# Turning batch 2 by DMA and loading batch 1 ahead of the second channel weight, in a sliding-window attention and MLP-mixer kernel

## The chip, the cores and the metric

The kernel runs on one core of a Trainium2 chip. Its time is the device time of one execution in microseconds (us), as the median of several runs. The engines are named as the profile names them: PE multiplies matrices (PEld loads its weights), DVE and ACT do elementwise work and read the matmul results out of PSUM, POOL does elementwise work on SBUF only, and SP issues most of the DMAs. POOL issues those DMAs that change fp32 weights to fp16 on the way. Each engine works through its own instructions in the order in which the program gives them, and waits for another engine or a DMA by a semaphore.

## The reference

Eight batches, eight heads, 576 positions of 64 elements. Half of the heads look back over a window of 32 positions, the other half over 128 positions in steps of four. The attention output is the input of an MLP mixer: a product over the positions, then one over the channels, each with a ReLU between two weights and a sum with its input.

```python
scores = scale * np.matmul(q, k.transpose(0, 1, 3, 2))
mask_plain = (rel >= 0) & (rel < 32)
mask_dil = (rel >= 0) & (rel < 128) & (rel % 4 == 0)
attn = softmax(where(mask, scores, -1e9));  x = attn @ v
h = np.maximum(xt @ w_tok1, 0.0) @ w_tok2          # positions
u = x + h.transpose(0, 2, 1)
out = u + np.maximum(u @ w_ch1, 0.0) @ w_ch2       # channels
```

The inputs are fp32; the kernel multiplies in fp16.

## The kernel before

The program has a start-up (batch 0's attention and position product, with nothing beside it) and then eight iterations, one for each batch `b`. The backbone of iteration `b` is the channel product of batch `b` on PE: twelve blocks `gp` (line 717, four matmuls of 512 columns each, a ReLU of each into `gt`), in odd iterations three small blocks `gt` and a block `yp` for the tails of two batches (lines 708 and 756), and four blocks `yp` against the second channel weight `w4` (line 736, 24 matmuls of 256 columns each). Into this backbone the program sets the attention and the position product of later batches. `interleave` does so by a table: each piece of side work has a place `t` on a counted time, and the pieces and the backbone are written out in that order. So the order on every engine is fixed when the program is built; the places are no waits.

A batch's side work is: loads of q, k and v (`l_q`, `l_k`, `lt` for the last 64 rows, `l_vn`, `l_vt`, `l_vd`, `l_vx`) issued by SP; casts to fp16 on POOL (`c_q`, `c_k`, `c_t`, `vv`, `vt`); q and k turned so that the head dimension lies on the partitions; scores, their exponentials on ACT (`attp` for the plain heads, `attd` for the dilated, `attt` for the last 64 queries); values (`av`, then `rec` and `xn` on DVE); position product (`h1p`, `up`, `u`); and `u` turned for the channel product (`uT`).

There are two ways to turn and to score. Batches 0 to 2 are turned by PE (`transposes`, line 310) and copied from PSUM; their scores are matmuls over 128 rows, in which the other head's rows are zero (`qz`). For batches 0 and 1 the mask is added by a further matmul (`veil`); for batch 2 POOL multiplies by the mask after the exponential. Batches 3 to 7 (`by_dma`) are turned by five DMA transposes on SP (`tt`, `qt`, `kr`, `qt`, `kr`; `qt` and `kr` are the places of q and k, two head pairs each time), POOL copies k into its place (`kt`, `place_steps`), and `scores_twin` computes two heads at once, each over 64 rows of PE, in two groups: group 0 for the plain heads, group 1 for the dilated. POOL multiplies by the masks after them. Their `u` is turned by a DMA transpose too (`turned`), into `utm`; ACT copies half of it into `utd` (line 649).

Loads are held back by a `gate`: a copy of one element on POOL into the tile that the first load writes, which can only run when the weight it reads has landed. Before the change the pieces of the first channel weight `w3` are loaded first, then a gate, the three pieces of `w4`, a gate on the first of them, and then batch 1.

Of the kernel before, what the change touches and what calls it, by code (L numbers as in the profile page):

```python
# [35 lines left out]
TW = 320  # L36
# [32 lines left out]
def kernel(  # L69
# [81 lines left out]
    w3a = fixed("w3", [128, 4, DCH])  # L151
    w3 = [w3a[:, i] for i in range(4)]
# [190 lines left out]
    def by_dma(b):  # L343
        return b >= 3
# [51 lines left out]
    def veiled(b, hp):  # L396
        return b <= 1
# [68 lines left out]
    def scores_twin(b, g):  # L466
# [35 lines left out]
        def main(hp):  # L502
            for h in range(2):
                p = ps[2 * (hp % 2) + h]
                if g == 0:
                    exp(plain_blocks(hp)[:, h, 0:3, 0:BLK].rearrange("p b (m r) -> p b m r", r=4),
                        p[:, 0:3 * BLK].rearrange("p (b r m) -> p b m r", r=4, m=40))
                else:
                    exp(attd[hp - 2][:, h], p)

        def rest():
            for h in range(2):
                p = small[h]
                if g == 0:
                    exp(attpa[:, :, h, 3 * PST:3 * PST + 128].rearrange("p a (m r) -> p a m r", r=4),
                        p[:, 256:512].rearrange("p (a r m) -> p a m r", a=2, r=4))
                t = attt[:, 2 * g:2 * g + 2, h, 64:TW].rearrange("p a (x c) -> p a x c", c=128)[:, :, :, 0:64]
                exp(t, p[:, 0:256].rearrange("p (a x c) -> p a x c", x=2, c=64))
# [9 lines left out]
        main(2 * g)  # L528
        if g:
            mask(2)  # L530
        main(2 * g + 1)
        if g:
            mask(3)
        rest()
        if not g:
            mask(0)
# [3 lines left out]
        if not g:  # L540
            mask(1)
# [89 lines left out]
    def turned(b):  # L631
        return b >= 3
# [18 lines left out]
    def score_steps(b, t0, dt, offs=(0.0, 0.7, 2.0), places=None):  # L651

        steps = []
        if by_dma(b):
            for g in range(2):
                for i, f in enumerate([scores_twin(b, g)] * 2):
                    steps.append((t0 + g * dt, 0.86 * (i == 0), lambda f=f: next(f)))
            return steps
        for hp in range(4):
# [4 lines left out]
            for i in range(3):  # L664
                steps.append((at_s + offs[i], 0.21, lambda g=g: next(g)))
# [30 lines left out]
    def gen_main(b):  # L696
# [4 lines left out]
        def w3_block(cb, mb):  # L701
            return w3[cb][:, 512 * (mb // 4) + mb % 4:512 * (mb // 4) + 512:4]
# [11 lines left out]
        for mb in range(NMB):  # L714
# [5 lines left out]
            relu(nc.vector if (mb % 2 == 1 if b == 0 else mb in (1, 5)) else nc.scalar, gta[:, mb, m0:m0 + 512], p)  # L720
# [86 lines left out]
    def load_w3(i):  # L807
        c = slice(512 * i, 512 * i + 512)
        nc.gpsimd.dma_start(out=w3a[:, :, c], in_=moe_w_ch1[:, c].rearrange("(x p) c -> p x c", p=128))
# [12 lines left out]
    nc.gpsimd.dma_start(out=w1p, in_=moe_w_tok1[0:512, :].rearrange("(m r) j -> m r j", r=4))  # L822
# [9 lines left out]
    load_w3(2)  # L832
# [90 lines left out]
    gate(w4a[0:1, 0, 0:1], w3[0][0:1, 512:513])  # L923
    for i in range(3):
        nc.gpsimd.dma_start(
            out=w4a[:, 4 * i:4 * i + 4],
            in_=moe_w_ch2[512 * i:512 * i + 512, :].rearrange("(p i) c -> p i c", i=4))
    gate(l32[(1, "t")][0:1, 0, 0:1], w4[0][0:1, 0:1])
    for nm in ("q", "k"):
        load_tail(1, nm, nc.sync)  # L930
    for h0 in (0, 4):
        for nm in ("q", "k"):
            load_qk(1, nm, h0, h0 + 4, nc.sync)
    casts1 = cast_steps(1)
    for i in (0, 1, 2, 3, 4, 5, 7, 6, 8):
        casts1[i]()
    load_v(1)
    new_qk(2)
    for nm in ("q", "k"):
        load_tail(2, nm, nc.sync)  # L940
    for nm in ("q", "k"):
        load_qk(2, nm, 0, 4, nc.sync)
# [4 lines left out]
    for b in range(B):  # L947
        steps = []
        if b == 0:
            steps += score_steps(1, 0, 0, (0.0, 0.6, 1.3),  # L950
                                 ((12.6, 14.8), (14.0, 16.8), (16.2, 18.6), (17.6, 20.2)))
            steps += at(18.6, 0.35, casts1[9:])
            steps += at(20.0, 0.0, [lambda nm=nm: load_qk(2, nm, 4, 8, nc.sync) for nm in ("q", "k")])
            steps += at(24.0, 0.0, [lambda: load_v(2)])
            casts = cast_steps(2)
            va = value_steps(1, 20.3, 0.7)
            steps += va[:4] + [(p + 0.2, c, f) for p, c, f in va[4:]]
            steps += mix_steps(1, 24.2, 27.0, 29.0, 34.8, 1.1)
            steps += score_steps(2, 0, 0, (0.0, 0.7, 1.6),
                                 ((28.8, 31.4), (31.2, 34.6), (0, 0), (0, 0)))[:10]  # L960
            steps += at(24.5, 0.5, casts[:9]) + at(34.5, 0.3, casts[9:])
            steps += at(36.0, 0.0, [lambda: emit_loads_qk(3)])
        elif b == 1:
            late = score_steps(2, -4.3, 2.4, (0.0, 0.7, 1.6))
            va = value_steps(2, 4.2, 1.0)
            steps += late[10:] + va[:4] + [(9.6 + (0.0, 0.8, 2.8, 3.6)[i], c, f) for i, (_, c, f) in enumerate(va[4:])]
# [44 lines left out]
```

## Time and profile before

| | |
|---|---|
| median of three runs | 293.93 us (293.59 to 293.98) |
| profiled execution | 293.95 us |
| its span, first to last instruction | 292.2 us |
| PE / PEld busy | 95% / 73% |
| DVE / ACT / POOL busy | 46% / 46% / 57% |
| DMA queue of SP, share of 16 engines | 64.8% |

The span begins with the first instruction of the kernel; 1.75 us of the profiled execution lie around it. The eight iterations begin at about 28.6, 69.7, 108.7, 138.1, 172.5, 201.2, 235.6 and 261.9 us. PE is busy nearly all the time, but its busy time is modelled and contains the tails of matmuls that overlap; what it loses is seen better in the waits and in the times at which its groups start.

### The profile page before, as it was taken

To read this page: it belongs to the slowest core of one execution; us is meant where nothing else is said; L and a number is where in the kernel's file an instruction comes from. 1 tells how busy PE (TensorE), PEld (TensorE's weight loads), DVE (VectorE), ACT (ScalarE), POOL (GpSimd) and SP (SyncE) were. 2 spreads that over 40 slices of the span, in tenths; PEclk is the share of its full clock that TensorE was granted. 3 is DMA by queue.
4 is the path that set the end of the run, shared out by engine and by line. 5 is a ranking of instruction groups with operands and counts; after the bars stand their busy time and mean duration, and the time that the engine had idled before them with its cause. 6 is when DMAs were issued, how large, how long until landed. Compare 5 with 4: busy or idle time off the path is not lost.

```text
span 292.2 us, 7087 instructions
## 1 busy us (share of the span) xinstructions
PE 278.1 (95%) x2850; PEld 213.4 (73%) x2850; DVE 133.2 (46%) x279; ACT 134.3 (46%) x266; POOL 166.3 (57%) x227
## 2 busy tenths in 40 slices
PE   5879999997999999999999999999999999999994
PEld 2677579985776896688766986697776966886593
DVE  7847338754844237413741245415540274422022
ACT  2854336347644614465347705482346524234500
POOL 7982056436999399739952998469952930000000
PEclk9999999999999999999999999999999999999999
DMA  8999999989938995869897989389775220431032
GB/s 222 271 202 190 206 323 210 328 220 276 245 64 183 306 264 131 103 118 329 238 181 139 326 208 217 73 210 336 193 145 100 84 72 2 90 111 36 2 90 91
DMA packets 103473, 52.12 MB, mean 178 GB/s; under 512 B 71792, under 2 KB 102384, under 8 KB 103440
## 3 DMA queue, kind: packets, MB, share of 16 engines
q1 hardware_dynamic: 99200, 46.55, 64.8%
q0 software_dynamic: 2640, 3.94, 7.7%
q10 hardware_dynamic: 1600, 1.18, 1.4%
q8 instruction: 22, 0.36, 0.5%
q14 instruction: 11, 0.09, 0.1%
HBM read 37.07 MB, written 9.44 MB: 159 GB/s over the span
## 4 chain that ended last, share of the span: by engine, by line
PE 84%; DMA 6%; POOL 5%; ACT 1%; SPq 1%; DVE 1%; issue 1%; POOLq 0%
PE yp L736 28%; PE gp L717 27%; PE h1p L579 5%; PE yp L756 4%; PE up L591 4%; PE gt L708 3%; DMA l_q<-in_q_dram 3%; DMA w1p<-in_moe_w_tok_dram 2%; PE sc L476 2%; PE h1p L577 1%; PE av L560 1%; PE up L602 1%; POOL vv L102 1%; PE av L555 1%; POOL attp L112 1%; DMA l_vd<-in_v_dram 1%
## 5 line engine op out<-in xcount | busy, mean ns | idle before, releaser
L736 PE MATMUL yp<-w,gt 128*128 128x256 f16 x756 | 86.9, 273 | 0.0
L106 ACT ACTIVATE gt<-gp 128x512 f16<-128x512 f32 x76 | 45.4, 597 | 84.4 <-PE gp L717 84.1
L736 PEld LDWEIGHTS <-gt 128*128 128x128 f16 x768 | 78.4, 106 | 6.5 <-issue 0.3
L717 PEld LDWEIGHTS <-w 128*128 128x128 f16 x384 | 40.0, 114 | 23.7 <-issue 1.5
L112 POOL TENSOR_TENSOR attp<-attp,const 128x1280 f16<-128x1280 f16 x12 | 31.3, 2611 | 33.7 <-ACT attp L500 27.5
L746 DVE TENSOR_TENSOR o<-yp,u 128x512 f32<-128x512 f32 x31 | 21.4, 691 | 62.3 <-PE yp L736 59.0
L717 PE MATMUL gp<-utd,w 128*128 128x512 f16 x120 | 45.5, 380 | 0.0
L717 PE MATMUL gp<-utm,w 128*128 128x512 f16 x120 | 45.5, 379 | 0.0
L717 PE MATMUL gp<-uT,w 128*128 128x512 f16 x144 | 36.3, 379 | 0.7 <-ACT uT L100 0.7
L112 DVE TENSOR_TENSOR xn<-av,rec 128x320 f16<-128x320 f32 x64 | 31.5, 492 | 2.2
L112 POOL TENSOR_TENSOR attd<-attd,const 128x1024 f16<-128x1024 f16 x12 | 25.3, 2123 | 0.0
L102 POOL CAST c_q<-l_q 128x512 f16<-128x512 f32 x31 | 19.7, 638 | 4.2 <-DMA l_q<-in_q_dram 4.2
L597 DVE TENSOR_TENSOR u<-up,xn 128x512 f16<-128x512 f32 x26 | 18.0, 691 | 8.1 <-PE up L591 8.1
L102 POOL CAST c_k<-l_k 128x512 f16<-128x512 f32 x29 | 17.7, 613 | 3.6 <-PE yp L736 1.8
L108 DVE TENSOR_SCALAR gt<-gp 128x512 f16<-128x512 f32 x20 | 13.8, 689 | 11.7 <-PE gp L717 11.2
L106 ACT ACTIVATE h<-h1p 128x256 f16<-128x256 f32 x29 | 11.1, 384 | 16.5 <-PE h1p L579 16.4
L568 DVE RECIPROCAL rec<-av 128x5 f32<-128x5 f32 x64 | 12.2, 190 | 13.2 <-PE av L565 12.7
L367 POOL COPY kt<-kr 128x512 f16<-128x512 f16 x10 | 10.8, 1078 | 7.9 <-DMA kr<-c_k 5.4
L500 ACT ACTIVATE attp<-sc 128x480 f16<-128x480 f32 (+1 forms) x30 | 13.4, 526 | 2.1 <-PE sc L476 2.1
L112 POOL TENSOR_TENSOR attt<-attt,const 128x512 f16<-128x512 f16 (+1 forms) x14 | 14.2, 1015 | 0.0
L393 PEld LDWEIGHTS <-kt 128*128 128x128 f16 x144 | 11.8, 103 | 3.2 <-issue 1.6
L606 DVE TENSOR_TENSOR u16t<-up,xn 64x512 f16<-64x512 f32 x7 | 4.8, 690 | 19.8 <-PE up L602 19.8
(136 smaller groups left out, 478.8 us busy)
## 6 DMA issues: line engine op xcount, KB each, us to landing
out_dram<-o SPq DMA_DIRECT2D x72, 128.0 KB, 3.4
l_q<-in_q_dram SPq DMA_DIRECT2D x15, 512.0 KB, 7.1
l_k<-in_k_dram SPq DMA_DIRECT2D x14, 512.0 KB, 7.3
l_vn<-in_v_dram SPq DMA_DIRECT2D x32, 128.0 KB, 5.3
l_vd<-in_v_dram SPq DMA_DIRECT2D x16, 256.0 KB, 4.7
w<-in_moe_w_ch_dram POOLq DMA_DIRECT2D x6, 512.0 KB, 7.6
lt<-in_q_dram SPq DMA_DIRECT2D x8, 128.0 KB, 4.5
l_vt<-in_v_dram SPq DMA_DIRECT2D x8, 128.0 KB, 4.1
```

Of the source, the lines that this page charges most:

```text
L102: eng.tensor_copy(out=out, in_=in_)
L106: nc.scalar.activation(out=out, in_=in_, func=AF.Relu)
L108: eng.tensor_scalar_max(out=out, in0=in_, scalar1=0.0)
L112: eng.tensor_tensor(out=out, in0=x, in1=y, op=ALU.mult)
L393: nc.tensor.matmul(out=out, lhsT=lhsT, rhs=qz[hp][:, h, queries], start=hide is None, stop=True)
L500: nc.scalar.activation(out=out, in_=in_, func=AF.Exp, scale=0.125)
L568: nc.vector.reciprocal(out=rec[:, :, 0], in_=av[:, :, 64])
L579: nc.tensor.matmul(out=p, lhsT=w[:, s, j], rhs=x[:, s, c], start=False, stop=(s == 3))
L597: nc.vector.tensor_tensor(out=u16(b, s), in0=blocks4(p), in1=blocks4(xn[b][:, s]), op=ALU.add)
L717: nc.tensor.matmul(out=p, lhsT=w3_block(cb, mb), rhs=uT[(b, cb)][0], start=(i == 0), stop=(i == 3))
L736: nc.tensor.matmul(out=p[:, c], lhsT=gta[:, mb, a0:m0 + 512:4] if half else gta[:, mb, a0:a0 + 128], rhs=w4[mb][:, c], start=(mb == 0), st ...
L746: nc.vector.tensor_tensor(out=blocks4(o32), in0=blocks4(p), in1=u16(b, s), op=ALU.add)
```

## The change

Batch 2 joins those that are turned by DMA (`by_dma` and `turned` from 2 on). Its scores move from the end of iteration 0 and the first third of iteration 1 to two places among the `gp` blocks of iteration 1, group 0 after the first block. The exponentials of `scores_twin` become single steps and begin with the small bank. The ReLUs of iteration 1 move in the greater part to DVE.

Batch 1 is loaded before `w4`: its gate now reads the second copy of `w2p` instead of `w4`. The third piece of `w3` is issued on POOL after two of batch 1's casts, the three pieces of `w4` after nine of them; `w3` is split into three tiles for that. Batch 1's transposes and scores move from the `yp` blocks of iteration 0 to its `gp` blocks, and its values and position product follow earlier. Batch 2's loads stand together, behind a gate on the second piece of `w4`. In the start-up, `w1p` is issued ahead of two casts.

```diff
     def by_dma(b):
-        return b >= 3
+        return b >= 2
...
     def turned(b):
-        return b >= 3
+        return b >= 2
...
+        def small_exps(h):
+            if g == 0:
+                last_blocks(h)
+                yield 0.0
+            tails(h)
+            yield 0.0
+
+        yield from small_exps(1)
+        for hp in (2 * g, 2 * g + 1):
+            for h in range(2):
+                main(hp, h)
+                if g and h:
+                    mask(hp)
+                yield 0.0
+        yield from small_exps(0)
+        if g == 0:
             mask(0)
...
-            relu(nc.vector if (mb % 2 == 1 if b == 0 else mb in (1, 5)) else nc.scalar, gta[:, mb, m0:m0 + 512], p)
+            relu(nc.vector if (mb % 2 == 1 if b == 0 else mb % 4 != 3 if b == 1 else mb in (1, 5)) else nc.scalar, gta[:, mb, m0:m0 + 512], p)
...
+    nc.gpsimd.dma_start(out=w1p, in_=moe_w_tok1[0:512, :].rearrange("(m r) j -> m r j", r=4))
+    for hp in range(2, 4):
+        cast_qk(0, "q", hp, nc.gpsimd)
     nc.gpsimd.dma_start(out=w1t[0][0:64], in_=moe_w_tok1[512:S, :])
     nc.gpsimd.tensor_copy(out=spread[:, 3:515:4], in_=ident)
-    for hp in range(2, 4):
-        cast_qk(0, "q", hp, nc.gpsimd)
-    nc.gpsimd.dma_start(out=w1p, in_=moe_w_tok1[0:512, :].rearrange("(m r) j -> m r j", r=4))
...
-    load_w3(2)
...
     new_qk(1)
-    gate(w4a[0:1, 0, 0:1], w3[0][0:1, 512:513])
-    for i in range(3):
-        nc.gpsimd.dma_start(
-            out=w4a[:, 4 * i:4 * i + 4],
-            in_=moe_w_ch2[512 * i:512 * i + 512, :].rearrange("(p i) c -> p i c", i=4))
-    gate(l32[(1, "t")][0:1, 0, 0:1], w4[0][0:1, 0:1])
+    gate(l32[(1, "t")][0:1, 0, 0:1], w2p[1][0:1, 0, 0:1])
...
+    load_v(1)
     casts1 = cast_steps(1)
-    for i in (0, 1, 2, 3, 4, 5, 7, 6, 8):
+    for i in (0, 1):
         casts1[i]()
-    load_v(1)
+    load_w3(2)
+    for i in (2, 3, 4, 5, 7, 6, 8):
+        casts1[i]()
+    for i in range(3):
+        nc.gpsimd.dma_start(
+            out=w4a[:, 4 * i:4 * i + 4],
+            in_=moe_w_ch2[512 * i:512 * i + 512, :].rearrange("(p i) c -> p i c", i=4))
+    for cast in casts1[9:]:
+        cast()
+
     new_qk(2)
+    gate(l32[(2, "t")][0:1, 0, 0:1], w4[4][0:1, 0:1])
     for nm in ("q", "k"):
         load_tail(2, nm, nc.sync)
-    for nm in ("q", "k"):
-        load_qk(2, nm, 0, 4, nc.sync)
+    for h0 in (0, 4):
+        for nm in ("q", "k"):
+            load_qk(2, nm, h0, h0 + 4, nc.sync)
+    load_v(2)
...
-            late = score_steps(2, -4.3, 2.4, (0.0, 0.7, 1.6))
-            va = value_steps(2, 4.2, 1.0)
...
-            steps += mix_steps(2, 10.8, 14.6, 17.2, 22.2)
-            steps += score_steps(3, 25.2, 4.2) + at(9.0, 0.6, cast_steps(3))
...
+            va = value_steps(2, 9.4, 0.95)
+            steps += score_steps(2, 0.6, 5.2, lag=0.5)
...
+            steps += mix_steps(2, 14.6, 18.4, 20.8, 32.8)
+            steps += score_steps(3, 27.0, 4.5) + at(9.0, 0.6, cast_steps(3))
```

Three places show how this moves the instructions. The first is POOL, from the end of the start-up on; the first number in a name is the number of the batch (`lt_1` belongs to batch 1). Before:

```order
L835 COPY w2p_1_83<-w2_81 128x512
L805 COPY w4_85<-w3_84 1x1
L925 DMA w4_85<-in_moe_w_ch2_dram 128x2048 x3
L805 CAST lt_1_583<-w4_85 1x1
L102 CAST c_t_1_595<-lt_1_583 128x512
L102 CAST c_q_1_597<-l_q_1_0_579 128x512
L102 CAST c_k_1_599<-l_k_1_0_581 128x512
```

Now:

```order
L842 COPY w2p_1_83<-w2_81 128x512
L813 CAST lt_1_584<-w2p_1_83 1x1
L102 CAST c_t_1_604<-lt_1_584 128x512
L102 CAST c_q_1_606<-l_q_1_0_580 128x512
L817 DMA w3_2_86<-in_moe_w_ch1_dram 128x4x512
L102 CAST c_k_1_609<-l_k_1_0_582 128x512
L102 CAST c_q_1_606<-l_q_1_0_580 128x512
L102 CAST c_k_1_609<-l_k_1_0_582 128x512
L102 CAST c_q_1_606<-l_q_1_1_581 128x512 x2
L102 CAST c_k_1_609<-l_k_1_1_583 128x512 x2
L944 DMA w4_87<-in_moe_w_ch2_dram 128x2048 x3
```

The gate of batch 1 stands ahead of all of `w4`, and the last third of `w3` and all of `w4` stand behind casts that wait for batch 1's data. After the rows shown come batch 1's casts of v, and only then the gate of batch 2.

The second place is SP's queue around batch 2's loads of v. Before:

```order
L191 DMA l_k_2_1_622<-in_k_dram 128x4x256
L752 DMA out_0_dram<-o32_0_2_906 128x256 x2
L208 DMA l_vn_2_1044<-in_v_dram 128x4x64 x4
L208 DMA l_vt_2_1047<-in_v_dram 64x8x64
L208 DMA l_vd_2_1045<-in_v_dram 128x2x256 x2
L208 DMA l_vx_2_1046<-in_v_dram 128x4x64
L752 DMA out_0_dram<-o32_0_3_1107 128x256 x2
L197 DMA lt_3_1275<-in_q_dram 64x8x64
```

Now:

```order
L207 DMA l_vd_2_641<-in_v_dram 128x2x256 x2
L207 DMA l_vx_2_642<-in_v_dram 128x4x64
L760 DMA out_0_dram<-o32_0_0_1016 128x256 x2
L348 DMA_TRANSPOSE tt_68<-c_t_2_1062 128x4x128
L760 DMA out_0_dram<-o32_0_1_1085 128x256 x2
L348 DMA_TRANSPOSE qt_66<-c_q_2_1064 128x8x128
L348 DMA_TRANSPOSE kr_67<-c_k_2_1081 128x8x128
L348 DMA_TRANSPOSE qt_66<-c_q_2_1064 128x8x128
L348 DMA_TRANSPOSE kr_67<-c_k_2_1081 128x8x128
L760 DMA out_0_dram<-o32_0_2_1153 128x256 x2
```

Batch 2's five transposes are new, and they stand behind all fourteen loads of the batch and behind the output of the first two blocks of iteration 0.

The third place is POOL in iteration 1, where k is put in place and the masks are applied. Before:

```order
L112 TENSOR_TENSOR attp_73<-attp_73,const_61 128x8x160
L112 TENSOR_TENSOR attt_76<-attt_76,const_61 128x2x2x64
L102 CAST vv0_69<-l_vn_2_1044 128x4x64 x4
L102 CAST vv0_69<-l_vt_2_1047 64x8x64
L102 CAST vv0_69<-l_vd_2_1045 128x4x2x64
L112 TENSOR_TENSOR attp_73<-attp_73,const_61 128x8x160
L112 TENSOR_TENSOR attt_76<-attt_76,const_61 128x2x2x64
```

Now:

```order
L366 COPY kt_65<-kr_67 128x512
L363 COPY kt_65<-tt_68 128x4x64
L366 COPY kt_65<-kr_67 128x512
L369 COPY kt_65<-kr_67 128x128 x2
L112 ISA
L112 TENSOR_TENSOR attp_73<-attp_73,const_61 128x8x160
L112 TENSOR_TENSOR attt_76<-attt_76,const_61 128x4x2x64
L112 TENSOR_TENSOR attp_73<-attp_73,const_61 128x8x160
L112 TENSOR_TENSOR attd0_74<-attd0_74,const_61 128x1024
L112 TENSOR_TENSOR attd1_75<-attd1_75,const_61 128x1024
L102 CAST c_t_3_1422<-lt_3_1244 128x512
L112 TENSOR_TENSOR attt_76<-attt_76,const_61 128x4x2x64
```

The copies of `kt` for batch 2 are new; where casts of v stood between the masks, all masks now stand in one run, with the mask of the dilated heads' tails last, behind a cast of batch 3.

More of the change, by code (lines that the diff above doesn't have):

```diff
@@ L150 @@
     w2p = [fixed(f"w2p_{i}", [128, 4, 128]) for i in range(2)]
-    w3a = fixed("w3", [128, 4, DCH])
-    w3 = [w3a[:, i] for i in range(4)]
+    w3 = [fixed(f"w3_{i}", [128, 4, 512]) for i in range(3)]
     w4a = fixed("w4", [128, NMB, DM])
@@ L655, in score_steps @@
             for g in range(2):
-                for i, f in enumerate([scores_twin(b, g)] * 2):
-                    steps.append((t0 + g * dt, 0.86 * (i == 0), lambda f=f: next(f)))
+                f = scores_twin(b, g)
+                at = t0 + g * dt
+                steps.append((at, 0.86, lambda f=f: next(f)))
+                for i in range(7 if g else 9):
+                    steps.append((at + lag * (i + 1), 0.0, lambda f=f: next(f)))
             return steps
@@ L664, in score_steps @@
             for i in range(3):
-                steps.append((at_s + offs[i], 0.21, lambda g=g: next(g)))
+                steps.append((at_s + offs[i], 0.42 if veiled(b, hp) else 0.21, lambda g=g: next(g)))
         return steps
```

71 lines of the change are left out of this document (28 added, 43 removed).

## The prediction

> **What bounds the kernel now.** I read the page's shares first, then the chain that ended last, then PE's waits, and then the stretches of time in which a wait stands.
>
> ```profile
> span 292.2 us, 7087 instructions
> PE 278.1 (95%) x2850; PEld 213.4 (73%) x2850; DVE 133.2 (46%) x279; ACT 134.3 (46%) x266; POOL 166.3 (57%) x227
> PE 84%; DMA 6%; POOL 5%; ACT 1%; SPq 1%; DVE 1%; issue 1%; POOLq 0%
> PEclk9999999999999999999999999999999999999999
> ...
> PE w_p L854 <- DMA w1p<-in_moe_w_tok_dram: 1.6, 1, 1.6
> ```
>
> PE is the bound: 84% of the chain is its work, and its clock is granted in every slice. Its one long wait is 1.6 us for `w1p` in the start-up. DMA (6%) and POOL (5%) enter the chain early. The windows (length, PE, PEld, DVE, ACT, POOL busy, then PE's clock, DMA share, GB/s) show what else is lost there:
>
> ```profile
> 24.00:36.00 12.00, 11.85 (x77) 7.36 (x76) 5.93 (x14) 4.42 (x9) 2.01 (x5) 1.00 1.08 198
> 36.00:45.00 9.00, 9.00 (x82) 7.16 (x81) 4.51 (x7) 3.04 (x6) 4.97 (x9) 1.00 1.13 299
> 45.00:47.00 2.00, 2.00 (x36) 1.99 (x34) 1.58 (x4) 1.39 (x4) 1.25 (x4) 1.00 0.73 160
> 47.00:60.00 13.00, 12.24 (x198) 11.55 (x196) 9.46 (x27) 5.26 (x12) 6.33 (x12) 1.00 1.01 291
> 60.00:72.00 12.00, 10.02 (x112) 8.12 (x111) 5.55 (x10) 9.03 (x20) 5.75 (x8) 1.00 0.87 237
> 72.00:81.00 9.00, 8.67 (x117) 6.23 (x116) 7.69 (x20) 4.89 (x10) 9.00 (x11) 1.00 0.95 252
> ```
>
> From 24 to 60 the DMA engines are full (a share of 1.0 or more) but for two microseconds. PE idles .76 + 1.98 + .33 = 3.1 us between 47 and 81. A change that needs loads earlier runs against the full queue; one that takes PE work away gains.
>
> **The change, part by part.** *PE's work.* These rows are the yardstick: an instruction's cost is the distance from one start to the next.
>
> ```profile
> 71.44 0.39 PE L310 MATMUL tp_q<-const,c_q 128*128 128x128 f16 x4
> 71.66 0.22 PE L328 MATMUL tp_q<-const,c_t 128*128 128x128 f16 x1
> ...
> 125.87 0.75 PE sc L476 x24
> 130.00 0.67 PE sc L476 x24
> 251.44 10.48 PE yp L736 x96
> 261.93 3.45 PE gp L717 x16
> ```
>
> A transpose costs .22/4 = .056; a `gp` block 3.45/4 = .863; a `yp` block 10.48/4 = 2.62. Gone are 36 transposes of batch 2 (2.0) and 16 of its `u` (.9); its 48 score matmuls, at .03 to .07 by their columns, cost 2.4, the twin groups .75 + .67, so about 1.0 is saved. Together **-3.9 us**.
>
> *Start-up.*
>
> ```profile
> 11.98 0.66 POOL L822 DMA_DIRECT2D w1p<-in_moe_w_tok_dram  x1
> ```
>
> `w1p` is now issued ahead of two casts and another load, at about 10.0 instead of 12.0, so the wait of 1.6 us and a little of the gap about it go: **-1.7**. The first `gp` starts at 26.9 instead of 28.6.
>
> *The loads.* What batch 2 needs now has to come through the full queue.
>
> ```profile
> 25.04 0.18 POOL L805 COPY w<-w 1x1 f16<-1x1 f16 x1 [4.00 <-DMA w<-in_moe_w_ch_dram]
> 25.52 1.65 POOL L925 DMA_DIRECT2D w<-in_moe_w_ch_dram  x3 [0.30 <-POOL w L805]
> 30.99 0.61 SPq L197 DMA_DIRECT2D lt<-in_q_dram  x1
> 46.01 0.47 SPq L208 DMA_DIRECT2D l_vx<-in_v_dram  x1
> 49.22 2.26 SPq L752 DMA_DIRECT2D out_dram<-o  x4
> 37.58 0.61 POOL L102 CAST c_t<-lt 128x512 f16<-128x512 f32 x1 [6.62 <-DMA lt<-in_k_dram]
> 50.21 0.41 POOL L102 CAST vt<-l_vx 128x256 f16<-128x256 f32 x1
> ...
> DMA to landing us min/median/max: 7.1/7.8/9.8
> ...
> DMA to landing us min/median/max: 5.2/7.3/9.5
> ```
>
> The last two rows are the landing times of the pieces of `w3` (line 809) and of `w4` (line 925). The second piece of `w3` landed at 25.0, where the gate ends; the third, issued at 18.26, 9.8 later at 28.0; `w4`, its last piece issued at 26.6, 9.5 later at 36.1; batch 1's last load at 50.2, just ahead of its cast. In the new order (batch 1, rest of `w3`, `w4`) the same bytes end at 50.2, or as early as 48 if the gap of 45 to 47 closes; I take 49.0. Behind them stand batch 2's fourteen loads. From 36.1, where `w4` was through, to 46.5, where SP had issued batch 1's last load, were 10.4 us; so SP issues batch 2's last load at 49.0 + 10.4 = 59.4.
>
> On SP the transposes follow: four outputs (2.26), `tt` and `qt`, then `kr`.
>
> ```profile
> 86.86 1.28 SPq L349 DMA_TRANSPOSE kr<-c_k  x1
> ...
> kr<-c_k SPq DMA_TRANSPOSE x10, 3.3
> ...
> 91.69 1.06 POOL L367 COPY kt<-kr 128x512 f16<-128x512 f16 x1
> 93.05 1.06 POOL L367 COPY kt<-kr 128x512 f16<-128x512 f16 x1
> 94.07 0.74 POOL L370 COPY kt<-kr 128x128 f16<-128x128 f16 x2
> ```
>
> A transpose takes SP 1.3 to issue: 59.4 + 2.26 + 2 x 1.3 = 64.3 for the issue of the first `kr`, 67.7 for its landing; POOL's copies for the plain heads take 94.07 - 91.69 = 2.4, to 70.1; the rest of twin group 0 takes .6. Call its end E: **E = 70.7**.
>
> PE would be there by itself at about 65.5. From 26.9 it has 36.3 of work: 13 `gp` blocks 11.2, 4 `yp` 10.5, of batch 1 transposes 2.0, scores 4.8 (masks added), values 1.8, `h1p` 2.2 and the rest 3.7. I add .3 for gaps and 2 for waits on ACT, whose exponentials of batch 1 now fall among the ReLUs. So PE waits some 5 us at group 0, a wait that the trace of before doesn't have; its bounds are 0 (loads soon enough) and 7 (the two added microseconds and more not needed). Behind it on PE stand all later blocks.
>
> *After group 0* come the exponentials and masks, as in the batch that before was the first turned by DMA.
>
> ```profile
> 96.62 2.24 ACT L500 ACTIVATE attp<-sc 128x480 f16<-128x480 f32 x5
> 99.23 0.45 ACT L500 ACTIVATE attt<-sc 128x256 f16<-128x256 f32 x1
> 99.56 2.61 POOL L112 TENSOR_TENSOR attp<-attp,const 128x1280 f16<-128x1280 f16 x1 [4.75 <-ACT attp L500]
> ...
> 109.99 1.16 POOL L112 TENSOR_TENSOR attt<-attt,const 128x512 f16<-128x512 f16 x1
> 111.10 0.61 POOL L102 CAST c_t<-lt 128x512 f16<-128x512 f32 x1
> 114.55 0.44 PE h1p L579 x4
> ...
> L649 ACT COPY utd<-utm 128x512 f16<-128x512 f16 x10 | 10.6, 1128 | 4.1 <-DMA utm<-u 4.1
> ```
>
> The exponentials took 99.56 - 96.62 = 2.9; with two more steps and a ReLU between, 3.8: masks start at E + 3.8 = 74.5. The masks took 111.10 - 99.56 = 11.5; with the cast that now stands ahead of the last, 12.1. The dilated tails are masked at 86.6. PE wants them at E + 12.3 = 83.0, by its blocks since E: it waits 3.6 there. From 86.6 it has 21.2 of work to the third iteration's first `gp`, at 108.1. There batch 3's chain is next: group 0 done at 100.8, masks from 103.7 to 115.3, while PE gets there at 114.0. With that wait of 1.3, and about 1.2 for the two copies `utd` (last row, 1.13 each on ACT, beside batch 3's exponentials), the `h1p` that ran at 114.55 runs at 116.5. All behind it is the same.
>
> *Sum.* +1.95 us on the profiled execution of 293.95 (span 292.2, and 1.75 around it); that lies .02 from the median of 293.93, so **295.9**. Put in another way, the two stalls (about 5 and 3.6) with the smaller waits give back more than the 3.9 of work, the 1.7 of `w1p` and the 3.1 of old idle time. As the chain from E on has no slack, the difference is E - 68.7: the kernel is faster if group 0 ends before 68.7.
>
> *Casts, ReLUs on DVE and small exponentials* I cost at nothing beside that: DVE and ACT are busy 46%, and they work under PE's blocks. Without that cover a late ReLU costs a `gp` block its bank for about .6 us, once in each place where exponentials stand amid ReLUs, which the 2 us above already hold for batch 1.
>
> **The rivals.** *Loads in time.* If the queue passes the same bytes some 4.3 us sooner, E is at PE's own 66.3 or so, and the time is 293.95 - 2.4 = 291.5; with all waits gone, 285 to 286. For it: from 36 to 45 the engines moved 299 GB/s, from 24 to 36 only 198, so a full queue may move more when the loads are mixed. Against it: what moved from 24 to 36 was mostly `w3` and `w4`, which change their type on the way, and these stay.
>
> *Slower yet by the gate.* POOL casts batch 1's v before it reaches batch 2's gate. If v is served behind `w4`, its casts end some 2.5 us after `w4`, and batch 2's loads start that much later: E = 73.2, 298.4. For it: batch 1's `lt`, issued from 30.99 on, reached its cast at 37.58, only after `w4`'s last piece of 36.1, as if served in order of issue. Against it: SP may issue v well ahead of POOL's `w4`. In "DMA: Bandwidth & Descriptors", section "Queues, rings and completion order", the Trainium skill says that each DMA engine goes round the queues that have work, a packet at a time; by that, v from SP's queue would land amid `w4`, and this rival would drop. The landing of `lt` speaks against it, though one row can't decide.
>
> *A cold clock.* Eight matmuls of 512 columns in the warm-up show what PE does at first:
>
> ```profile
> 2.54 3.59 PE L784 MATMUL idle_p<-idle 128*128 128x512 f16 x8 [2.54 <-POOL idle L161]
> ```
>
> 3.59/8 = .45 each against .216 later. No wait of before is over 1.6 us, so the trace can't say whether a stall of 5 brings that rate back; if each of two stalls costs some .9 (four matmuls at the slow rate), the time is 297.7. The Trainium skill ("TensorE: Matmul & The Clock Gate", "Part 1: The HAM clock gate") has the clock halved after an idle window of about 3.4 us; both stalls that I forecast are over that.
>
> *No difference.* A queue quicker by 1.3 to 2.5 us puts E at 68.2 to 69.4, and the time within 0.2% (.6 us, about what this kernel's measurement can tell from no change).
>
> **How the numbers follow.** Forecast as worked out .36; gate .10; cold clock .08; loads in time .31; no difference .15. So slower .54, same .15, faster .31. The forecast's own range is 294.6 to 297.5, E from 69.4 to 72.2, from the ends 48 and 50.2 of the queue and the two microseconds on PE. As cases of both signs hold most of the chance, the range reaches from 290.8 (loads in time, and part of the second stall gone) to 299.0 (late gate).
>
> **What would show it.** In the profile after: the wait of PE for `w1p` gone and the first `gp` near 26.9; the first `kr` of batch 2 issued near 64.3, its copies into `kt` on POOL done near 70.1; a wait of PE at batch 2's first twin scores (`sc`) on POOL's `kt` of some 5 us, and one at `av` on POOL `attt` of 3.6; the third iteration beginning near 110. The forecast is wrong if batch 2's last load is issued before 57, if PE comes to group 0 after its keys, or if PEclk drops in a slice between 60 and 90. If the masks end by E + 12 without PE waiting, the second stall was put too high.

## The result and the profile after

| | before | after |
|---|---|---|
| median of the runs | 293.96 us (4 runs) | 302.55 us (4 runs, 301.66 to 303.57) |
| ratio, 95% interval | | 1.0296 (1.0262 to 1.0331) |
| span of the profiled execution | 292.2 us | 299.9 us |

The changed kernel is slower, by 8.6 us where 2.0 were forecast. Medians here and below are over all executions of a kernel; a ratio leaves out those over 1.5% above the kernel's fastest, which concerns two of the four of one kernel below (304.74 and 305.98). The page of the changed kernel, by the same lines as before:

```profile
span 299.9 us, 6922 instructions
PE 277.3 (92%) x2798; PEld 210.4 (70%) x2798; DVE 132.2 (44%) x274; ACT 127.7 (43%) x253; POOL 168.1 (56%) x230
PEclk9999998999997999999999999999999999999999
PE 75%; DMA 11%; issue 4%; POOL 3%; SPq 2%; DVE 1%; ACT 1%; ACTq 0%; POOLq 0%; DVEq 0%
```

PE has 52 matmuls fewer, as reckoned, but its share of the chain fell from 84 to 75%, that of the DMAs rose from 6 to 11%, and in two slices its clock was not granted whole. PE's longest waits but for the start-up's (engine, line, releaser: total, times, longest):

```profile
PE av L568 <- POOL vt L102: 4.4, 1, 4.4
PE av L568 <- POOL attt L112: 2.8, 1, 2.8
PE gp L725 <- ACT utd L654: 2.6, 1, 2.6
PE sc L475 <- POOL kt L366: 1.5, 2, 0.9
```

Of the first three the kernel before has the second alone, with 0.3. Where they stand in PE's timeline:

```profile
49.69 0.19 PE L568 MATMUL av<-vt,attt 128*128 128x65 f16 x1 [4.43 <-POOL vt L102]
73.99 0.44 PE L475 MATMUL sc<-qt,kt 64*128 64x160 f16 x8 [0.95 <-POOL kt L366]
90.49 0.20 PE L568 MATMUL av<-vt,attt 128*128 128x65 f16 x1 [2.79 <-POOL attt L112]
116.32 0.38 PE L725 MATMUL gp<-utd,w 128*128 128x512 f16 x1 [2.58 <-ACT utd L654]
```

The third iteration begins at 116.3 (before: 108.7), and the loss stays: the last iteration's first blocks begin at 270.0, where 261.9 were seen before (chain of waits):

```profile
270.03 3.45 PE gp L725 x16
```

The first wait is for the last load of batch 1's v. POOL's timeline shows what it holds up:

```profile
35.14 1.61 POOL L944 DMA_DIRECT2D w<-in_moe_w_ch_dram  x3
49.23 0.40 POOL L102 CAST vt<-l_vx 128x256 f16<-128x256 f32 x1 [4.86 <-DMA l_vx<-in_v_dram]
49.58 0.18 POOL L813 CAST lt<-w 1x1 f32<-1x1 f16 x1
71.55 1.06 POOL L366 COPY kt<-kr 128x512 f16<-128x512 f16 x1 [5.86 <-DMA kr<-c_k]
```

POOL issued `w4` at 35.1; that load of v was cast at 49.2, and batch 2's gate stands behind the cast. So SP starts batch 2's loads only then:

```profile
34.88 1.73 SPq L207 DMA_DIRECT2D l_vx<-in_v_dram  x1
49.78 0.61 SPq L196 DMA_DIRECT2D lt<-in_q_dram  x1
60.95 0.47 SPq L207 DMA_DIRECT2D l_vx<-in_v_dram  x1
62.54 1.36 SPq L348 DMA_TRANSPOSE tt<-c_t  x1
65.93 0.82 SPq L760 DMA_DIRECT2D out_dram<-o  x2
68.17 1.27 SPq L348 DMA_TRANSPOSE kr<-c_k  x1
107.13 5.97 SPq L644 DMA_TRANSPOSE utm<-u  x1
```

The windows (length, PE, PEld, DVE, ACT, POOL busy, PE's clock, DMA share, GB/s) show the DMA engines empty behind the late gate, and the clock at half behind two of the waits:

```profile
49.50:50.50 1.00, 0.81 (x7) 0.43 (x7) 0.52 (x2) 0.00 (x0) 0.25 (x2) 0.74 0.00 0
50.50:51.50 1.00, 1.00 (x9) 0.50 (x8) 0.97 (x4) 0.00 (x0) 0.00 (x0) 0.50 0.17 39
51.50:52.50 1.00, 1.00 (x5) 0.40 (x4) 0.43 (x1) 0.00 (x0) 0.00 (x0) 0.50 0.72 164
52.50:53.50 1.00, 1.00 (x12) 0.80 (x11) 0.49 (x2) 0.60 (x1) 0.00 (x0) 0.56 0.61 124
91.00:93.00 2.00, 2.00 (x14) 1.37 (x13) 1.07 (x3) 0.28 (x1) 2.00 (x4) 0.50 0.17 33
93.00:95.00 2.00, 2.00 (x16) 1.39 (x14) 1.21 (x4) 0.48 (x2) 2.00 (x5) 0.66 0.78 149
```

Worked out from the rows (1 less the clock, times the length, over one half), each slow stretch lasted 3.4 us; PE lost half of that, 1.7. Behind the wait of 2.6 at 116.3 the clock stayed whole.

### The profile page after: what moved, and what is told of

Read it like the earlier page. It is cut to its first block, busy times and chain, and to the rows that moved or that the text cites. A ratio compares the mean times of both kernels' runs of the same rounds, so it can differ in the third digit from the quotient of the medians.

```text
span 299.9 us, 6922 instructions
## 1 busy us (share of the span) xinstructions
PE 277.3 (92%) x2798; PEld 210.4 (70%) x2798; DVE 132.2 (44%) x274; ACT 127.7 (43%) x253; POOL 168.1 (56%) x230
## 4 chain that ended last, share of the span: by engine, by line
PE 75%; DMA 11%; issue 4%; POOL 3%; SPq 2%; DVE 1%; ACT 1%; ACTq 0%; POOLq 0%; DVEq 0%
PE gp L725 25%; PE yp L744 23%; PE h1p L584 5%; PE up L596 4%; PE yp L764 4%; DMA l_vd<-in_v_dram 3%; PE gt L716 3%; DMA utm<-u 3%; DMA lt<-in_k_dram 2%; DMA l_vt<-in_v_dram 2%; PE sc L475 2%; PE h1p L582 1%; POOL attd L112 1%; PE av L565 1%; DMA kr<-c_k 1%
## 5 line engine op out<-in xcount | busy, mean ns | idle before, releaser
L106 ACT ACTIVATE gt<-gp 128x512 f16<-128x512 f32 x69 | 41.2, 597 | 76.3 <-PE gp L725 75.9
L725 PE MATMUL gp<-utd,w 128*128 128x512 f16 x144 | 54.7, 380 | 2.7 <-ACT utd L654 2.6
L725 PE MATMUL gp<-utm,w 128*128 128x512 f16 x144 | 54.6, 379 | 0.0
L725 PE MATMUL gp<-uT,w 128*128 128x512 f16 x96 | 26.4, 397 | 0.0
L499 ACT ACTIVATE attp<-sc 128x480 f16<-128x480 f32 (+1 forms) x36 | 15.9, 535 | 19.1 <-PE sc L475 19.1
L108 DVE TENSOR_SCALAR gt<-gp 128x512 f16<-128x512 f32 x27 | 18.6, 688 | 12.0 <-PE gp L725 11.6
L366 POOL COPY kt<-kr 128x512 f16<-128x512 f16 x12 | 12.8, 1068 | 11.3 <-DMA kr<-c_k 11.2
L654 ACT COPY utd<-utm 128x512 f16<-128x512 f16 x12 | 12.6, 1120 | 6.2 <-DMA utm<-u 6.2
L112 POOL TENSOR_TENSOR attt<-attt,const 128x512 f16<-128x512 f16 x12 | 13.9, 1155 | 0.0
L768 DVE TENSOR_TENSOR o<-yp,u16t 128x512 f32<-128x512 f32 x4 | 2.8, 692 | 24.2 <-PE yp L764 24.2
```

The source lines that it names most:

```text
L106: nc.scalar.activation(out=out, in_=in_, func=AF.Relu)
L108: eng.tensor_scalar_max(out=out, in0=in_, scalar1=0.0)
L112: eng.tensor_tensor(out=out, in0=x, in1=y, op=ALU.mult)
L366: nc.gpsimd.tensor_copy(out=natural(kt[hp][:, 0:512]), in_=kra[:, hp].rearrange("p r m -> p m r"))
L499: nc.scalar.activation(out=out, in_=in_, func=AF.Exp, scale=0.125)
L654: nc.scalar.copy(out=natural(uTd[:, cb - 2]), in_=uTm[i][:, cb].rearrange("p r m -> p m r"))
```

## The experiments

Each line gives the median, and the ratio to the kernel before with its 95% interval. Fifteen kernels ran.

**Four single edits.** The first puts `w4` two casts later on POOL:

```
+    for cast in casts1[9:11]:
+        cast()
     for i in range(3):
         nc.gpsimd.dma_start(out=w4a[:, 4 * i:4 * i + 4], ...)
-    for cast in casts1[9:]:
+    for cast in casts1[11:]:
```

> The changed kernel, with one edit: POOL issues the three pieces of w4 behind the first two casts of batch 1's v instead of ahead of all of them, so that SP has all fourteen loads of batch 1 in the queue before w4. Theory A (the last two loads of batch 1's v are served behind w4; this holds PE at the dilated tails' values for 4.6 us, takes the clock away for another 1.6, and holds batch 2's gate on POOL until 49.6): the wait of PE on vt at 45 is gone, no slow clock near 50, batch 2's first load issued near 46.5 instead of 49.8, batch 2's group 0 done near 69 to 71 instead of 74.6, and the time 296 to 299. Theory B (what binds is the chain of batch 2's transposes and masks, whatever comes before it): group 0 stays near 74, and the time within 1.5 us of 302.5.

302.47 us, 1.0311 (1.0268 to 1.0355): no effect, and no test of either theory, since the two casts had their data and the issue moved by 0.4 us only. (Here PE waited 3.2 us for `utd` at 117.0, and the clock stayed whole behind that.) POOL's timeline of this kernel:

```profile
35.54 1.62 POOL L946 DMA_DIRECT2D w<-in_moe_w_ch_dram  x3
48.83 0.41 POOL L102 CAST vt<-l_vx 128x256 f16<-128x256 f32 x1 [7.47 <-DMA l_vx<-in_v_dram]
```

The second masks the dilated tails first (`small_exps(0)` and the mask of `attt` ahead of the loop over `hp` for `g == 1`).

> The changed kernel, with one edit: in group 1 the exponentials of both tails come first, and POOL masks the dilated tails ahead of the two masks of the dilated heads (for every batch that is turned by DMA). Theory A (PE stands 2.95 us at 87.5 because that mask stands last, behind a cast, and loses 1.6 more by the slow clock after it): that wait falls under 1 us, the clock stays whole at 91 to 94, and the time is 298 to 299.5. Theory B (what is won there is waited for again at the third iteration's start, where the copies utd come late by the DMA queue): the wait at 113.5 grows from 2.7 to 5 or more, and the time is above 301.

301.27 us, 1.0272 (1.024 to 1.0304). PE's waits:

```profile
PE gp L727 <- ACT utd L656: 3.5, 1, 3.5
PE av L567 <- POOL attd L112: 0.8, 2, 0.6
```

The wait at the values fell as theory A says, from 2.8 to 0.8, and the third iteration began 1.7 earlier (114.6); the wait for `utd` grew by 0.9 of it. So the time is between the two theories. Behind the wait of 3.5 us for `utd`, too, the clock stayed at 1.00.

The third is `at(27.0, 0.7, load_steps(4))` in place of `at(22.0, 0.9, load_steps(4))`.

> The changed kernel, with one edit: batch 4's loads are placed from 27.0 on (0.7 apart) instead of from 22.0 (0.9 apart), so that SP issues the transpose of batch 2's u ahead of them. Theory A (PE stands 2.7 us at the third iteration's start since that transpose waits 8 us behind six loads): the wait goes, and the time is 299.5 to 300.3. Theory B (the transpose waits for u itself, or the later loads hold a later batch): 302 or more.

302.18 us, 1.0283 (1.0256 to 1.0309). PE's wait for `utd` is gone, but there are two waits for the mask now, the new one of 1.8 us at batch 3's values, so rival B in its second form, and the last iteration begins at 269.98, as before this edit:

```profile
PE av L568 <- POOL attt L112: 4.5, 2, 2.8
```

The fourth has only the start-up's edit on the kernel before.

> The kernel before, with one part of the change alone: w1p is issued ahead of two casts and another load. As forecast, the wait of 1.6 us goes and is carried to the end: 292.2 to 292.7. Rival: what PE wins is waited for again between 47 and 72, where the full DMA queue sets when batch 1 and 2 are there: 293.4 to 294.

293.95 us, 1.0005 (0.9986 to 1.0025). The wait for `w1p` is gone from PE's waits, and another stands there that was not:

```profile
PE gp L717 <- DMA w<-in_moe_w_ch_dram: 0.7, 1, 0.7
```

PE now waits for the first piece of `w3`. In the profiled execution the last iteration begins 0.85 us earlier; in the median of ten executions no gain can be told.

**The load that came late, taken out of the way.** `w4` behind four casts of v (`casts1[9:13]`), so issued at 39.2:

> The changed kernel, with w4 issued behind the first four casts of batch 1's v (near 39.6), so that the last load of v, whose issue SP ends at 36.3, is in the queue well ahead of w4; putting w4 behind two casts had moved its issue by only 0.4 us, and that load still landed with w4's third piece. Theory A (that load's place behind w4 makes the stall of 4.6, the slow clock after it and the late gate): no wait of PE on vt at 45, the clock whole near 50, batch 2's first load issued near 47, group 0 done at 69 to 71 instead of 74.6, the time 297 to 299. Theory B (SP's and the DMA engines' work for batch 2 binds from wherever it starts): PE's stall moves to batch 2's scores, group 0 at 73 or later, the time above 300.5.

303.25 us; the ratio, 1.0249 (1.0203 to 1.0294), compares 299.86 and 301.75 with the kernel before. The mechanism of theory A came out: no wait on `vt`, batch 2's first load issued at 47.2, `kr` here:

```profile
64.83 1.29 SPq L348 DMA_TRANSPOSE kr<-c_k  x1
```

PE reached the second iteration at 64.6 instead of 71.1 and group 0 ended near 71.7. But the time hardly fell: the profiled execution took 301.75 against 301.66, and the intervals of the two ratios overlap. PE's waits:

```profile
PE sc L475 <- POOL kt L366: 4.4, 2, 3.7
PE gp L725 <- ACT utd L654: 3.2, 1, 3.2
PE av L568 <- POOL attt L112: 2.8, 1, 2.8
```

and windows behind the first and the second of these three:

```profile
71.00:73.00 2.00, 2.00 (x20) 1.07 (x17) 0.00 (x0) 1.23 (x4) 0.51 (x2) 0.50 0.57 171
117.00:119.00 2.00, 2.00 (x15) 0.95 (x13) 0.55 (x2) 0.60 (x1) 2.00 (x3) 0.51 0.95 247
```

Of the 6.5 us that PE won at the second iteration's start, 1.3 were left at the third's (115.0 against 116.3), and none at the last one's. The wait at the scores grew by 2.9, and the clock ran at half behind all three waits, from within the first one on for 6.8 us. So the late load was one way to the loss, and not its ground.

The three repairs together (`w4` behind four casts, tails' mask first, batch 4's loads later):

> The kernel with w4 behind four casts of v, with the mask of the dilated tails first in group 1, and with batch 4's loads from 27.0 on: the three repairs together. If the stalls add up along one chain, as theory A has it: the stall at the dilated tails' values under 1 us, the one at the third iteration's start near 0.5, and the time 292.5 to 294.5. If what one repair wins is waited for at the next place (rival): above 297.

298.13 us, 1.0147 (1.0114 to 1.018): above 297, as the rival has it. Yet the three together are worth 1.5% of the time, where singly they were worth 0.5, 0.2 and 0.1%. PE waits 6.2 us for `kt` here, in three pieces, 4.5 of them at batch 2's first scores.

**Turning alone, and the place of the scores.** The kernel before, with `by_dma` and `turned` from 2 on and the changed kernel's table for the second iteration, but the old loads and start-up:

> The kernel before, with batch 2 turned by DMA and scored by the twin scores at the changed kernel's places in the second iteration, but with the loads, the start-up and batch 1's places as they were before. Theory A (the order of the loads costs the changed kernel most of its loss; batch 2's keys are there by 68 here): group 0 done at 68 to 70, no stall over 3 us before it, the time 292 to 296. Rival (turning batch 2 by itself gives a chain of transposes and masks that PE has to wait for): 298 or more.

299.77 us, 1.0218 (1.0196 to 1.0241): the rival. PE's waits:

```profile
PE sc L476 <- POOL kt L367: 4.4, 2, 3.4
PE gp L717 <- ACT utd L649: 2.8, 1, 2.8
```

They are two of the three of the kernel with the new loads and the late load out of the way (there 4.4 and 3.2); the mask `attt` costs 0.6 here, where it cost 2.8. So turning batch 2, with its scores right at the start of the iteration, is slower by itself. The same two kernels were then run with batch 2's work later in that iteration. On the new loads (`w4` behind four casts, tails' mask first):

```
-            va = value_steps(2, 9.4, 0.95)
-            steps += score_steps(2, 0.6, 5.2, lag=0.5)
+            va = value_steps(2, 12.0, 0.9)
+            steps += score_steps(2, 3.0, 4.4, lag=0.4)
```

> The kernel with w4 behind four casts of v and the dilated tails' mask first, and with batch 2's scores, values and position product placed later in the second iteration (group 0 from 3.0 instead of 0.6, group 1 4.4 behind it, values from 12.0, batch 3's casts from 12.6, batch 4's loads from 30.0). Theory A (PE has other work enough in that iteration to cover batch 2's transposes and masks, and the table put them too early for it): no stall over 1 us between 60 and 105, the time 289 to 292. Rival (u then comes too late for the third iteration, which waits for utd instead): a wait of 2 us or more near 108, the time 293 to 297.

293.97 us, 1.0026 (1.0 to 1.0052). The same on the old loads:

> The kernel before with batch 2 turned by DMA alone (299.77 us: loads, start-up and batch 1's places as before), and batch 2's scores, values and position product placed later in the second iteration, as in the kernel that came to 293.97. Theory A (what a turned batch costs is PE's wait for its keys and masks, since the table puts its scores right at the start of the iteration; the new order of the loads is not needed for it): the waits of 3.8 and 1.1 at the scores fall to under 2 together, the time is 293 to 296. Rival (without the loads' new order the keys or u are late anyway): 298 or more.

296.21 us, 1.0073 (1.0038 to 1.0108). The place is worth 4.2 us on the new loads (from 298.13, with batch 4's loads and batch 3's casts moved along) and 3.6 on the old (from 299.77). The first stayed above theory A's 289 to 292, since PE still waits; in its four waits for `kt` two are at batch 2:

```profile
PE sc L475 <- POOL kt L366: 4.2, 4, 1.9
PE gp L727 <- ACT utd L656: 1.0, 1, 1.0
```

**The clock by itself.** In the kernel with three repairs, PE is given matmuls that nobody uses while it waits for batch 2's keys, first 14, then 24 of them:

```
+        if b == 2 and g == 0:
+            for _ in range(24):
+                nc.tensor.matmul(out=ps[0], lhsT=idle[:, 0:128], rhs=idle, start=True, stop=True)
```

> The kernel with the three repairs (w4 behind four casts of v, the dilated tails' mask first, batch 4's loads from 27.0 on; 298.13 us), and with 14 matmuls of 512 columns into a bank that batch 2's first scores then overwrite, so that PE works for some 3 us of the wait of 4.9 for batch 2's keys (it computes nothing that is used). Theory A (that wait costs not only itself, but 1.6 us more, since the clock is granted at half for about 3.3 us after it): group 0 ends when it did, the clock is whole from 69 to 75, and the time falls by about 1.6 us, to 296.5. Rival (the clock is not lost by the wait, or what is lost is waited for anyway): the same time, 298.

297.48 us, 1.0117 (1.008 to 1.0155). The executions ran from 295.00 to 299.20, and the profiled one is the slowest, so the time decides nothing. In its timeline 14 left two waits, of 1.95 and 0.94 us, and the clock was at half for 3.4 us behind them. The kernel of 293.97 us has the same two waits at the same place, and its clock stayed whole. For each, the first wait and the window behind them, first with the 14, then the kernel of 293.97:

```profile
70.03 0.38 PE L475 MATMUL sc<-qt,kt 64*128 64x160 f16 x6 [1.95 <-POOL kt L366]
72.00:74.00 2.00, 2.00 (x17) 0.82 (x12) 0.00 (x0) 1.54 (x5) 0.30 (x1) 0.50 0.54 146
```

```profile
69.63 0.38 PE L475 MATMUL sc<-qt,kt 64*128 64x160 f16 x6 [1.90 <-POOL kt L366]
72.00:74.00 2.00, 2.00 (x23) 1.49 (x22) 0.77 (x2) 2.00 (x6) 0.00 (x0) 1.00 0.52 127
```

With 24 of them (the expectation puts the waits that 14 left at 3.5; in the timeline they are the 1.95 and 0.94):

> The kernel with the three repairs (298.13 us), and with 24 matmuls of 512 columns, some 5.2 us, ahead of batch 2's first scores, where PE waited 4.9 and 1.1 us. 14 of them had left a wait of 3.5 us, and the clock was still lost for some 3.3 us after it. Theory A (a wait costs its own length and, from some 3 us on, 1.6 us or more by the slow clock behind it): now no wait over 1.2 us is left there, the clock stays whole from 65 to 80, group 0 ends when it did, and the third iteration begins 1.6 to 2.5 us earlier than the 111.2 of the kernel it is made from. Rival (the slow stretch hides behind what PE waits for anyway): the third iteration begins at 111 as before.

298.04 us, 1.0151 (1.0126 to 1.0177). The same window without (first row) and with the 24 (second):

```profile
72.00:74.00 2.00, 2.00 (x21) 1.22 (x22) 0.00 (x0) 0.97 (x3) 0.73 (x2) 0.50 0.55 176
```

```profile
72.00:74.00 2.00, 2.00 (x26) 1.23 (x23) 0.54 (x1) 1.46 (x5) 0.31 (x1) 1.00 0.57 161
```

The clock stays whole, and the third iteration begins at 108.5 instead of 111.2, 2.6 earlier and a little more than theory A's bound. So a wait can cost more than itself. At batch 4's scores PE then waits 2.5 us, 1.5 more than without, and the last iteration begins 1.1 earlier (265.2 against 266.3). In the median nothing is left: only two of the six executions show a mean clock of 1.00 (296.80 and 297.20); four show 0.994 and took 297.97 to 299.45. Where those four lost the clock was not recorded.

**SP's order.** From the kernel with the later place on, batch 2's `tt`, `qt`, `kr` stand ahead of the last four loads of v and ahead of all outputs, and k is put in place ahead of the last casts of v:

```
-    load_v(2)
+    loads_v2 = load_v_steps(2)
+    for step in loads_v2[:4]:
+        step()
...
+            steps += at(21.0, 0.0, casts[:5] + turns2[:3] + loads_v2[4:])
```

> The kernel with w4 behind four casts of v, the dilated tails' mask first and batch 2's work later in the second iteration, and with one more edit: on SP the transposes tt, qt and kr of batch 2's plain heads stand ahead of the last four loads of v and ahead of all outputs of the first iteration, and POOL puts k in place before the last casts of v; the scores move back to 1.6, the values to 10.4, batch 4's loads go around the transpose of u. Theory A (in the kernel it is made from, PE waits 2.1 + 1.1 us for keys that SP issues at 65.1, behind all loads of v and four outputs; they could be issued near 58.5): kr issued by 60, no wait over 1 us at batch 2's scores, group 0 done near 67, and the time 289 to 291.5. Rival (the DMA engines are what binds: the transposes wait in the queue for the loads ahead of them, or v now comes too late for the masks' engine): the wait turns up at the values or the third iteration's start, and the time is 293 or more.

293.6 us, 0.9983 (0.9958 to 1.0008). PE has no wait of over half a microsecond from 16 to 91, and the third iteration begins at 104.2, 4.4 earlier than in the kernel before. All of it is lost again by the last iteration (262.1 against 261.9): 2.3 in waits at batch 4's scores, and 1.7 by the clock, which was at half for 3.4 us from 124.5 on, behind these waits of 1.4 and 0.9; where the rest goes is not shown. The three executions with a mean clock of 0.999 took 291.21 to 293.23, the other nine 292.60 to 294.95. PE's waits, those at batches 3 and 4 in the first row:

```profile
PE sc L475 <- POOL kt L366: 5.0, 4, 1.7
PE gp L727 <- ACT utd L656: 1.0, 1, 1.0
```

The next kernel does the same for batch 3, and loads batch 4's q and k ahead of the transpose of batch 2's u:

> The kernel with batch 2's first three transposes ahead of its last loads of v (293.6 us), and with the same done for batch 3, whose loads of q and k also move from behind all outputs of the first iteration to behind two of its four blocks; batch 4's loads of q and k stand ahead of the transpose of batch 2's u. Theory A (in the kernel it is made from, PE has no wait at batch 2 any more and begins the third iteration at 104.2, 4.3 earlier than the kernel before, but waits 3.1 us at batch 3's scores, 1.2 at utd and 2.6 at batch 4's scores, each time for keys whose loads and transposes SP issued late): these waits go for the greater part, the third iteration begins by 101.5 and the time is 286.5 to 290. Rival (POOL, busy without a gap from 69 to 90, or the full DMA engines set when batch 3's keys are there, whatever SP's order): the waits stay, the time is 292 or more.

296.6 us, 1.0105 (1.008 to 1.0131), a miss. `kr` of batch 3 was issued 2.8 earlier, but POOL's copies stood behind casts of v that now came later, and the loads ahead of the transpose of u made PE wait:

```profile
PE gp L727 <- ACT utd L656: 4.6, 1, 4.6
PE sc L475 <- POOL kt L366: 2.8, 2, 1.9
```

With both mended (copies ahead of those casts, the transpose of u ahead of batch 4's loads, batch 3's loads of q and k ahead of the first iteration's outputs, batch 4's transposes right behind their casts):

> The kernel with batch 2's first transposes ahead of its last loads of v (293.6 us), with the waits that it has left at batches 3 and 4 attacked in one: batch 3's loads of q and k stand right behind batch 2's transposes and ahead of all outputs of the first iteration, its transposes of the plain heads are issued as soon as their five casts are done, and POOL puts its k in place ahead of the last casts of v; the same for batch 4's transposes; the transpose of batch 2's u stands ahead of all loads of batch 4, and its copies utd ahead of the exponentials of batch 3's group 1. Theory A (SP's order is what makes keys and u late, and engines and queue have room): PE waits under 1 us at batch 3's scores, at utd and at batch 4's scores, the third iteration begins by 102 and the time is 287 to 290. Rival (POOL's masks and casts, which ran without a gap from 69 to 90, set when batch 3's keys are there): the wait at batch 3's scores stays at 2 us or more, the time 292 to 295.

292.37 us, 0.9939 (0.9905 to 0.9973). PE's waits for `kt` are 3.0 in three pieces, two of them at batch 4. The last edit (`turns4` are batch 4's transposes, `ld4` its loads, of which the last four are v's):

```
-            steps += at(27.2, 0.4, load_steps(4))
+            steps += at(27.2, 0.4, ld4[:10])
...
-                    steps += at(2.0, 0.6, casts[:5]) + at(4.5, 0.0, turns4[:3])
+                    steps += at(2.0, 0.6, casts[:5]) + at(4.5, 0.0, turns4[:3] + ld4[10:])
```

> The kernel of 292.37 us, with one more edit: the last four loads of batch 4's v stand behind its transposes of the plain heads instead of ahead of them. Theory A (PE's last waits of 1.2 and 1.1 us, at batch 4's scores, come from kr issued at 118.5 behind those loads, though its casts were done by 113.7; it can go by 116): the wait falls by 2 us, and the time to 290.3. Rival (the queue is full there, or the next batch waits instead): the same time within 0.7 us.

290.56 us, 0.9892 (0.9872 to 0.9913): 1.1% faster than the kernel before, the fastest of all. Its page and its longest wait but those of the start-up:

```profile
span 288.1 us, 6920 instructions
PEclk9999999999999999999999999999999999999999
```

```profile
PE sc L475 <- POOL kt L366: 1.9, 3, 0.9
```

## Why the prediction was wrong

The direction held, the size did not, and the direction held in part for another reason: the wait of some 5 at group 0 was 1.5 only, since PE itself came there at 72.1 and not at 65.5. Four terms failed, and they can be read off two places of the changed kernel's timeline, the end of group 0 (E) and the third iteration's start.

1. **The loads, E = 70.7.** Measured 74.6 (73.99 and the 0.61 that PE took there). The step "SP issues batch 2's last load at 49.0 + 10.4 = 59.4" took the queue as full; it ran empty, since POOL's gate stood behind the cast of a load that landed with `w4`. That is the second rival, put at .10 and priced at E = 73.2; the issue ended at 61.4, 2.0 late. What neither step held is that PE itself needs this v: its wait of 4.4, and the slow clock behind it, made PE and a block of outputs late, and SP waited from 63.9 to 65.9 for that block, ahead of `qt` and `kr`. 2.0 + 2.0 are the 3.9, but for rounding. With the load out of the way, SP did not wait there, and the forecast's own chain came out: PE at group 0 at 65.7 (forecast 65.5), `kr` at 64.8 (64.3), PE's wait at group 0 of 4.4 ("some 5"), at the tails 2.8 (3.6). From E to the last mask, too, it was 15.9 as forecast (74.6 to 90.5).

2. **The clock.** Set aside as a rival with .08, at .9 for each stall. From E on it cost 1.7, behind the wait of 2.8. The Trainium skill ("TensorE: Matmul & The Clock Gate", "Part 1: The HAM clock gate") has half the rate after an idle window of some 3.4 us, in windows that run freely beside the program. The rate agrees (0.50), and so do the stretches, 3.4 and 6.8 us long. The length of the wait does not: 2.8 us was enough at 90 us, and elsewhere 1.4 and 0.9 one behind the other, while 3.2 and 3.5 at the third iteration's start in two other kernels were not. So by these runs the length of a wait alone doesn't tell.

3. **The copies `utd`, "about 1.2" for the two.** Measured 2.6 for the first. The step looked at ACT; what is late is the transpose of u, which SP issues at 107.1 behind six loads of batch 4 and which takes until 115.2. With those loads later, PE's wait there was gone.

4. **Batch 3's wait of 1.3.** It did not come, since PE was later than forecast and batch 3's masks were there. With the wait for `utd` taken away, one of 1.8 came.

The working puts the third iteration's start at 108.1 (its list of signs says near 110; and 86.6 + 21.2 is 107.8, though 21.5 of work is what the trace shows there). It began at 116.3, and 3.9 + 1.7 + 2.6 = 8.2 is that difference. This is 7.7 later than in the kernel before; .4 more came behind it, where 2.5 were forecast (1.3 and 1.2): 8.1 in all, which is the distance at the last iteration (270.0 and 261.9). The span grew by 7.7, and the profiled execution, 301.66, lies .9 under the median.

**-3.9 of PE's work** was not measured by itself. PE's busy time, which is modelled, is 278.1 before and 274.7 to 276.1 in the four kernels in which batch 2 is turned by DMA, nothing is filled in and PE's clock is whole in every slice of the page: 2.0 to 3.4 lower. **-1.7 of the start-up** came as 1.3 at the first `gp` (27.3 against 28.6) and is wrong as a gain at the end: alone it is not to be told from zero. 0.7 of it is waited for again at the next weight; where the rest goes is not shown. **The sentence "the difference is E - 68.7"** is what fell furthest. Moving E by 2.9 (74.6 to 71.7) left the start of the last iteration where it was (270.15 and 270.03), since clock lost behind the waits comes on top of them, and later steps (u, loads) have their own reasons to be late.

Costing the ReLUs on DVE at nothing was not tested apart. With turning alone at the later place, where they stay as before the change, PE has a wait of 1.1 for a ReLU in the second iteration, which the kernel of 293.97 us does not have.

On the rule of the Trainium skill weighed in the second rival ("DMA: Bandwidth & Descriptors", "Queues, rings and completion order": a DMA engine goes round its queues a packet at a time): by it v would have landed amid `w4`. It did not: issued at 34.9, it reached its cast at 49.2, with `w4`'s last piece, and in the kernel where `w4` was issued 0.4 later again. Only with `w4` issued at 39.2 did it come through, 7.1 us after its issue. Why it was served so late is not settled; that SP took 1.73 us to issue it may bear on it, and was not tried apart.

## What to carry to other kernels

A fixed order takes work out of one engine only where the table also says when the other engines can have the result: first find the earliest time of the slowest feeder (here SP's transpose behind its own loads and outputs), then set the consumer behind it. SP issues in the program's order (the transpose of u stood behind six loads until 107.1), so what an engine waits for goes ahead of what only has to be done some time (v, outputs, the next batch's loads). When a wait is taken away, look for the same microseconds at the next place before counting them: here a place three batches on had to be served before the gain could be seen at the end.

## What was not expected of the hardware

- Behind a wait the clock was granted at 0.50 for 3.4 us, or for twice that; filling the wait with unused matmuls kept it at 1.00 there. How long the wait was did not decide it: it happened behind 1.4 and 0.9 us in a row, and did not behind 3.5.
- The transpose of u, issued behind six loads, kept SP for 5.97 us and took until 115.2 to be read by ACT, 8.1 us after its issue; the twelve transposes `kr` of the same kernel landed after 3.2 us in the median.
